# x, v, pos_emb and the result in the order of the kernel's loads and stores

## The chip, the core and the metric

One NeuronCore of a Trainium2 chip runs the whole program. Its engines are TensorE (PE; PEld is its weight load), VectorE (DVE), ScalarE (ACT), GpSimd (POOL) and SyncE (SP); in this kernel SP issues every DMA, one after the other. The metric is the time of one execution on the device, in microseconds. What the host does to the arrays before and after the execution is not in it.

## What is computed

A gated long convolution over the sequence (batch 4, sequence 12480, 128 channels) and then a token-wise network with a hard-swish between its two matrices:

```python
h_filt = (np.maximum(pos_emb @ w1, 0.0) @ w2) * window      # S x 128, window = exp(-0.01 pos)
u = x * v                                                   # B x S x 128
y = irfft(rfft(u, n=2*S) * rfft(h_filt, n=2*S))[:, :S]      # causal convolution over the sequence
a = (x * y).reshape(B * S, 128)
h = a @ w_in                                                # 128 -> 2048
out = (h * np.clip(h + 3.0, 0.0, 6.0) / 6.0) @ w_out        # 2048 -> 128
```

## The kernel before

The sequence is laid out as 196 rows of N1 = 64 positions (98 and 97 of them hold data, for the halves k = 0 and 1, called R[0] and R[1]); the Fourier transform over it is done by matmuls in stages. The program has three parts, one after the other.

**The filter (`Conv.filter`).** `pos_emb` is loaded with one of the 98 rows on each partition into the tile z (called `pt` there, the rows of k = 0 and k = 1 side by side). For 16 groups of NB = 4 positions `turned` transposes it on TensorE (L293, four transposes into one bank) and VectorE copies the bank out (L300), and `hidden` multiplies by w1 (L305) and applies ReLU on ScalarE (L306); a group is turned two groups ahead of its `hidden`. `spread` multiplies by w2 (L327) and by the window on VectorE (L335). Then come the first transform stage (L223, evicted at L235 and L233) and the second (L242), and the filter's spectra are stored to `hd` in memory (L351). All this is done for 64 of the 128 channels at a time. The tables `ftab`, `ctab`, `dtab` and the first pieces of x and v are loaded meanwhile.

**The convolution (`Conv.period`).** There are NG = 8 periods, each for 2 of the 4 sequences and G = 32 channels, and each has 25 chunks of up to four frequencies. A chunk runs `spectra` (L242, with a table piece `tab`), `swapped` (L474 and L475 on ScalarE, into the one bank of `sw`), `products` (L495 to L498 on VectorE with a filter piece `h`, then the sums L502 on GpSimd) and, two chunks later, `third_stage` (L517, copied out at L525). In between, periods 1 to 7 turn the period before back (`back`, L532, L136, L137; `fourth_stage`, L551, L557; `store`), and periods 0 to 6 run the first stage of the period after (`visit`, eight of them, L223 and L235).

For that first stage `gate_next` multiplies x by v on GpSimd (L426), and `load_next` loads the next x and v (L415). A load covers half the positions of one piece (98 rows of 32 positions by 32 channels), and each position's 32 channels are a run of 128 bytes in memory:

```python
part = slice(half * N1 // 2, (half + 1) * N1 // 2)
for t, src in ((xt, self.x), (vt, self.v)):
    for r0, r1 in ((0, 96), (96, R[k])):
        nc.sync.dma_start(t[r0:r1], self.rows(src, b, k, r0, r1)[:, part, d : d + G])
```

Each period makes eight such loads, four DMAs each. In the same queue of SP stand, for each chunk, two DMAs of `h` (L459, NH = 4 buffers) and one of `tab` (L446, NT = 7 buffers), each issued when a buffer comes free, and the stores of y (L567, L569). SP takes its rows strictly in the order of the program: a DMA that waits for its buffer, or for an earlier DMA on the same semaphore, holds all behind it.

**The network (`Moe`).** 98 tiles of 512 tokens; a tile's x and y are loaded (`load`), multiplied (`gate`), transposed by 32 x 32 blocks on VectorE (`turn`), put through both matrices by matmuls in three passes (`up`, L764 to L766; `down`, L799 to L803), transposed back (`finish`, L816) and stored. Its x load and its result store go through `copy`, by four DMAs of 32 partitions each (32 DMAs for a tile of leftover rows), in runs of 32 channels:

```python
for q in range(4):
    s = tile[32 * q : 32 * q + 32, cols].rearrange("r (n c) -> r n c", c=32)
```

## Time and profile before

| | |
|---|---|
| three runs | 3316.59, 3317.9 and 3318.12 us, median 3317.9 us |
| the profiled execution | 3315.44 us, of which 3313.7 us from the first to the last instruction |
| busy: PE, PEld | 3226.8 us (97%), 2764.7 us (83%) |
| busy: DVE, ACT, POOL | 2380.8 us (72%), 2400.2 us (72%), 2108.6 us (64%) |
| DMA packets | 972127, of which 841962 under 512 bytes; 296.41 MB |

The page is one execution. Its busy times are sums over three parts with different limits, so a part is read by itself: the filter stands in the first 171 us, the convolution up to about 1185 us, and the network after that. A matmul's end is modelled, so that a busy PE is not always one at its peak. The profiled execution is 2.5 us under the median of the runs.

### The profile page before, as it was taken

How to read it: one execution, taken by the hardware profiler on the slowest of the kernel's cores; microseconds unless marked ns; L12 is line 12 of the kernel's file. 1: busy time of each engine (PE TensorE's matmuls, PEld its weight loads, DVE VectorE, ACT ScalarE, POOL GpSimd, SP SyncE). 2: the span in 40 equal slices, each digit the busy share in tenths (PEclk: the TensorE clock that was granted, in tenths of full speed). 3: DMA queues.
4: the chain of work that ended last, by engine and by line, in shares of the span. 5: the costliest groups of instructions: out<-in, count | busy, mean ns of one | idle time of the engine just before them, and what ended most of it. 6: DMA issues, size and time to landing. Idle time of an engine off the chain costs nothing.

```text
span 3313.7 us, 54920 instructions
## 1 busy us (share of the span) xinstructions
PE 3226.8 (97%) x20346; PEld 2764.7 (83%) x20346; DVE 2380.8 (72%) x2837; ACT 2400.2 (72%) x3104; POOL 2108.6 (64%) x1243
## 2 busy tenths in 40 slices
PE   8988999999999999999999999999999999999999
PEld 7988888888888888888888888888888888888887
DVE  5545666666766667777777777777777777777776
ACT  2355666666667677778778787787878777777777
POOL 1166677676776546666666666666666666666666
PEclk9998999999999999999999999999999999999999
DMA  9789989989985522211211222112221112221121
GB/s 208 200 163 187 187 186 193 187 194 186 189 186 168 170 61 39 39 33 34 45 34 34 39 39 39 34 34 38 39 39 37 32 37 39 39 39 32 36 39 23
DMA packets 972127, 296.41 MB, mean 89 GB/s; under 512 B 841962, under 2 KB 938641, under 8 KB 970769
## 3 DMA queue, kind: packets, MB, share of 16 engines
q1 hardware_dynamic: 971860, 292.91, 42.1%
q8 instruction: 160, 2.62, 0.4%
q14 instruction: 107, 0.88, 0.1%
HBM read 224.49 MB, written 68.29 MB: 88 GB/s over the span
## 4 chain that ended last, share of the span: by engine, by line
PE 68%; POOL 0%; DVE 0%; issue 0%; ACT 0%
PE acc L803 11%; PE ph L764 11%; PE acc L800 11%; PE ph L765 11%; PE acc L799 11%; PE ph L766 11%; PE s L551 1%; PE ts L532 1%; PE s L517 1%; PE s L242 1%; PE s L532 0%; POOL pa L502 0%; DVE o L816 0%; ACT oT L806 0%; DVE wlo L137 0%
## 5 line engine op out<-in xcount | busy, mean ns | idle before, releaser
L788 POOL TENSOR_TENSOR glo<-g,ghi 128x1024 fp32r<-128x1024 f32 x588 | 1404.3, 2395 | 766.5 <-ACT ghi L786 766.3
L776 DVE SCALAR_TENSOR_TENSOR g<-r,ph 128x1024 f32<-128x1024 f32 (+1 forms) x784 | 949.5, 1211 | 411.1 <-ACT r L774 411.0
L774 ACT ACTIVATE r<-ph,three 128x1024 f32<-128x1024 f32 (+1 forms) x784 | 870.9, 1111 | 274.1 <-PE ph L766 274.0
L786 ACT CAST ghi<-g 128x1024 fp32r<-128x1024 f32 (+1 forms) x784 | 811.0, 1034 | 0.8 <-DVE g L776 0.7
L764 PE MATMUL ph<-xhi,win_hi 128*128 128x512 f32 (+1 forms) x1568 | 608.4, 388 | 0.0
L765 PE MATMUL ph<-xlo,win_hi 128*128 128x512 f32 (+1 forms) x1568 | 608.3, 388 | 0.0
L766 PE MATMUL ph<-xhi,win_lo 128*128 128x512 f32 (+1 forms) x1568 | 608.3, 388 | 0.0
L800 PE MATMUL acc<-ghi,wout_lo 128*128 128x512 f32 (+1 forms) x1568 | 608.0, 388 | 0.0
L799 PE MATMUL acc<-ghi,wout_hi 128*128 128x512 f32 (+1 forms) x1568 | 607.9, 388 | 0.0
L502 POOL TENSOR_TENSOR pa<-pa,pq 128x256 f32<-128x256 f32 (+1 forms) x400 | 312.5, 788 | 274.7 <-DVE pa L496 234.3
L803 PE MATMUL acc<-glo,wout_hi 128*128 128x512 f32 (+1 forms) x1568 | 481.2, 388 | 0.0
L764 PEld LDWEIGHTS ph<-xhi,win_hi 128*128 128x128 f32 x1568 | 294.3, 188 | 60.9 <-DVE g L776 0.2
L799 PEld LDWEIGHTS acc<-ghi,wout_hi 128*128 128x128 f32 x1568 | 294.4, 188 | 60.7
L765 PEld LDWEIGHTS ph<-xlo,win_hi 128*128 128x128 f32 x1568 | 294.5, 188 | 60.5
L766 PEld LDWEIGHTS ph<-xhi,win_lo 128*128 128x128 f32 x1568 | 294.4, 188 | 60.5
L800 PEld LDWEIGHTS acc<-ghi,wout_lo 128*128 128x128 f32 x1568 | 294.3, 188 | 60.4
L803 PEld LDWEIGHTS acc<-glo,wout_hi 128*128 128x128 f32 x1568 | 293.5, 188 | 60.9 <-POOL glo L788 0.7
L495 DVE TENSOR_TENSOR pq<-s,h 128x256 f32<-128x256 f32 (+1 forms) x200 | 84.2, 421 | 284.2 <-issue 106.3
L788 DVE TENSOR_TENSOR glo<-g,ghi 128x1024 fp32r<-128x1024 f32 x196 | 283.6, 1447 | 0.0
L223 PEld LDWEIGHTS ts<-ctab,u 98*64 98x64 f32 (+1 forms) x5120 | 229.4, 139 | 46.4 <-DVE wlo L137 24.9
L223 PE MATMUL ts<-ctab,u 98*64 98x99 f32 (+1 forms) x5120 | 246.8, 254 | 21.3 <-DVE wlo L137 20.8
L517 PE MATMUL s<-pa,tab 128*128 128x128 f32 x1694 | 240.9, 288 | 26.7 <-POOL pa L502 14.8
(72 smaller groups left out, 4060.0 us busy)
## 6 DMA issues: line engine op xcount, KB each, us to landing
tab<-in_g_tab SPq DMA_DIRECT2D x192, 256.0 KB
h<-hd SPq DMA_DIRECT2D x384, 128.0 KB
xt<-in_x SPq DMA_DIRECT2D x64, 384.0 KB
vt<-in_v SPq DMA_DIRECT2D x64, 384.0 KB
yd<-y SPq DMA_DIRECT2D x192, 128.0 KB
xt<-in_x SPq DMA_DIRECT2D x384, 64.0 KB
yt<-yd SPq DMA_DIRECT2D x96, 256.0 KB
out<-o SPq DMA_DIRECT2D x384, 64.0 KB
```

Source lines behind the costliest of these rows:

```text
L223: nc.tensor.matmul(tv[c * N1 : (c + 1) * N1, i, :K2], u[: R[k], 4 * j + i, :], self.ctab[: R[k], c * K2 : (c + 1) * K2], start=True, stop= ...
L502: nc.gpsimd.tensor_tensor(out=x, in0=x, in1=y, op=add)
L764: nc.tensor.matmul(ph[:, i, :ne], self.win_hi[:, sl], hi[:, :ne], start=True, stop=False)
L765: nc.tensor.matmul(ph[:, i, :ne], self.win_hi[:, sl], lo[:, :ne], start=False, stop=False)
L766: nc.tensor.matmul(ph[:, i, :ne], self.win_lo[:, sl], hi[:, :ne], start=False, stop=True)
L774: nc.scalar.activation(r[:, :, :ne], ph[:, :, :ne], AF.Relu, bias=self.three)
L776: nc.vector.scalar_tensor_tensor(out=g[:, :, :ne], in0=r[:, :, :ne], scalar=6.0, in1=ph[:, :, :ne], op0=ALU.min, op1=ALU.mult)
L786: nc.scalar.copy(ghi[:, :, :ne], g[:, :, :ne])
L788: e.tensor_tensor(out=glo[:, :, :ne], in0=g[:, :, :ne], in1=ghi[:, :, :ne].bitcast(F32), op=ALU.subtract)
L799: nc.tensor.matmul(a, self.wout_hi[:, f, :], ghi[:, i, :ne], start=(f == 0), stop=False)
L800: nc.tensor.matmul(a, self.wout_lo[:, f, :], ghi[:, i, :ne], start=False, stop=False)
L803: nc.tensor.matmul(a, self.wout_hi[:, f, :], glo[:, i, :ne], start=False, stop=(f == NFC - 1))
```

## The change

The host hands x, v and `pos_emb` over in the order in which the kernel's tiles hold them, x a second time (`xt`) in the order of the network's tiles, and takes the result in that order too.

- `by_groups`: x and v by period, piece and half, so that a half now is 16 channels with all 64 positions; a partition's share of a load is one run of 4096 bytes. The tile has the order of u, and both halves k have 98 rows (the rows beyond the sequence are zeros). The gate's output is no longer strided.
- `by_pairs`: `pos_emb` with 128 values (64 features of two positions) on the partitions. The transposes, their copies and the two memsets of the padding go; `hidden` reads the loaded tile. It is loaded in four pieces (4, 12, 16 and 32 positions), after w1 and ahead of `ident`.
- `by_tiles` and `from_tiles`: a tile's x load and its result store are one DMA of 128 partitions by 2048 bytes each. The y load is as before.

```diff
+def blocks(a):
+
+    b, s, d = a.shape
+    out = np.zeros((b, 2 * L, d), a.dtype)
+    out[:, :s] = a
+    return out.reshape(b, 2, R[0], N1, d)
+
+
+def by_groups(a):
+
+    a = blocks(a).reshape(B // GB, GB, 2, R[0], N1, D // G, 2, G // 2)
+    a = a.transpose(0, 5, 2, 1, 6, 3, 7, 4)
+    return np.ascontiguousarray(a).reshape(NG, 2 * GB, 2, R[0], G // 2, N1)
+
+
+def by_tiles(a):
+
+    a = blocks(a)
+    main = a[:, :, : 32 * NR].reshape(B, 2, NR, 32, N1 // 16, 16, 4, 32).transpose(0, 1, 2, 4, 6, 3, 5, 7)
+    main = main.reshape(-1, 128, 512)
+    rest = np.stack([a[i] for i in REST]).reshape(-1, 2, 32, 4, 32).transpose(3, 2, 0, 1, 4).reshape(128, -1)
+    pad = np.zeros((128, -rest.shape[1] % 512), a.dtype)
+    rest = np.concatenate([rest, pad], axis=1).reshape(128, -1, 512).transpose(1, 0, 2)
+    return np.ascontiguousarray(np.concatenate([main[:AT], rest, main[AT:]]))
+
+
+def from_tiles(t):
+
+    n = -(-len(REST) // 8)
+    main = np.concatenate([t[:AT], t[AT + n :]])
+    out = np.zeros((B, 2, R[0], N1, D), t.dtype)
+    out[:, :, : 32 * NR] = (
+        main.reshape(B, 2, NR, N1 // 16, 4, 32, 16, 32).transpose(0, 1, 2, 5, 3, 6, 4, 7).reshape(B, 2, 32 * NR, N1, D)
+    )
+    rest = t[AT : AT + n].transpose(1, 0, 2).reshape(4, 32, -1, 2, 32)[:, :, : len(REST)].transpose(2, 3, 1, 0, 4)
+    for i, a in zip(REST, rest.reshape(-1, N1, D)):
+        out[i] = a
+    return np.ascontiguousarray(out.reshape(B, 2 * L, D)[:, :S]).reshape(B * S, D)
+
+
+def by_pairs(a):
+
+    a = blocks(a[None])[0].reshape(2, R[0], N1 // 4, 2, 2, FO)
+    return np.ascontiguousarray(a.transpose(4, 5, 2, 0, 3, 1)).reshape(2 * FO, N1, R[0])
...
@@ -265,53 +307,25 @@
 
         flat = z.rearrange("p k c -> p (k c)")
 
-        pt = flat[: R[0], : 2 * N1 * FO].rearrange("p (k n i) -> p k n i", k=2, n=N1)
-        pos = [pos_emb[k * L : k * L + R[k] * N1, :].rearrange("(r n) i -> r n i", n=N1) for k in range(2)]
-
-        def load_pos(n0, n1):
-            for k in range(2):
-                nc.sync.dma_start(pt[:96, k, n0:n1, :], pos[k][:96, n0:n1, :])
-
-        nc.vector.memset(pt[96 : R[0], 1, :NB], 0.0)
-        nc.gpsimd.memset(pt[96 : R[0], 1, NB:], 0.0)
-        load_pos(0, NB)
-        nc.sync.dma_start(self.ident, ident_d)
-        for k in range(2):
-            nc.sync.dma_start(pt[96 : R[k], k], pos[k][96:])
+        pT = flat[:, : N1 * R[0]].rearrange("p (n r) -> p n r", r=R[0])
         for k in range(2):
             nc.sync.dma_start(w1bd[k * FO : (k + 1) * FO, k * FO : (k + 1) * FO], w1)
-        for n in ((NB, 8), (8, 16), (16, 32), (32, N1)):
-            load_pos(*n)
+        for n0, n1 in ((0, NB), (NB, 16), (16, 32), (32, N1)):
+            nc.sync.dma_start(pT[:, n0:n1, :], pos_emb[:, n0:n1, :])
+        nc.sync.dma_start(self.ident, ident_d)
         for k in range(2):
             nc.sync.dma_start(w2bd[k * FO : (k + 1) * FO, k, :], w2)
         nc.sync.dma_start(win, win_d)
         nc.sync.dma_start(self.ctab, self.c_tab)
 
-        def turned(n):
-            tp = self.bank("ptT")
-            for i in range(NB):
-                nc.tensor.transpose(
-                    tp[:, i * R[0] : (i + 1) * R[0]],
-                    pt[:, i // 2, n + i % 2 * 2 : n + i % 2 * 2 + 2, :].rearrange("p n i -> p (n i)"),
-                    self.ident[: R[0], : R[0]],
-                )
-            i = 2 * N1 * FO + n // NB % 4 * NB * R[0]
-            pT = flat[:, i : i + NB * R[0]]
-            nc.vector.tensor_copy(pT, tp[:, : NB * R[0]])
-            return pT
-
-        def hidden(n, pT):
+        def hidden(n):
             h1 = self.bank("h1")
-            nc.tensor.matmul(h1[:, : NB * R[0]], w1bd, pT, start=True, stop=True)
+            src = pT[:, n : n + NB, :].rearrange("p n r -> p (n r)")
+            nc.tensor.matmul(h1[:, : NB * R[0]], w1bd, src, start=True, stop=True)
             nc.scalar.activation(ht[:, n : n + NB, :].rearrange("p n r -> p (n r)"), h1[:, : NB * R[0]], AF.Relu)
 
-        pend = []
         for n in range(0, N1, NB):
-            pend.append((n, turned(n)))
-            if len(pend) > 2:
-                hidden(*pend.pop(0))
-        while pend:
-            hidden(*pend.pop(0))
+            hidden(n)
 
         for q in range(3):
             nc.sync.dma_start(ftab[:, 33 * q : 33 * q + 33, :], f_tab[:, 33 * q : 33 * q + 33, :])
...
@@ -407,25 +421,21 @@
             return
         g, i = divmod(self.n_loaded, 4 * GB)
         piece, half = divmod(i, 2)
-        k, b, d = self.place(g, piece)
-        xt, vt = ((xv or self.xv).tile([R[0], N1 // 2, G], F32, tag=f"{c}t", name=f"{c}t") for c in "xv")
-        part = slice(half * N1 // 2, (half + 1) * N1 // 2)
+        xt, vt = ((xv or self.xv).tile([R[0], G // 2, N1], F32, tag=f"{c}t", name=f"{c}t") for c in "xv")
         for t, src in ((xt, self.x), (vt, self.v)):
-            for r0, r1 in ((0, 96), (96, R[k])):
-                nc.sync.dma_start(t[r0:r1], self.rows(src, b, k, r0, r1)[:, part, d : d + G])
-        self.loaded.append((k, part, xt, vt, xv is None))
+            for r0, r1 in ((0, 96), (96, R[0])):
+                nc.sync.dma_start(t[r0:r1], src[g, piece, half, r0:r1])
+        self.loaded.append((half, xt, vt, xv is None))
         self.n_loaded += 1
 
     def gate_next(self):
 
         if self.loaded:
-            k, part, xt, vt, again = self.loaded.pop(0)
-            if part.start == 0:
+            half, xt, vt, again = self.loaded.pop(0)
+            if half == 0:
                 self.gated.append(self.up.tile([R[0], G, N1], F32, tag="u", name="u"))
-            u = self.gated[-1]
-            self.nc.gpsimd.tensor_tensor(
-                out=u[: R[k], :, part].rearrange("p g n -> p n g"), in0=xt[: R[k]], in1=vt[: R[k]], op=ALU.mult
-            )
+            u = self.gated[-1][:, half * G // 2 : (half + 1) * G // 2, :]
+            self.nc.gpsimd.tensor_tensor(out=u, in0=xt, in1=vt, op=ALU.mult)
             if again:
                 self.load_next()
 
...
-        self.tiles[16:16] = [REST[i : i + NB // 2] for i in range(0, len(REST), NB // 2)]
+        self.tiles[AT:AT] = [REST[i : i + NB // 2] for i in range(0, len(REST), NB // 2)]
         self.loaded, self.gated, self.ready, self.done = {}, {}, {}, None
 
...
     def columns(self, t):
         return 64 * len(self.tiles[t]) if self.is_rest(t) else 32 * self.NB
 
-    def places(self, arr, t):
-
-        NB, i = self.NB, self.tiles[t]
-        if self.is_rest(t):
-            for s, (b, k, r) in enumerate(i):
-                a = arr[b, k * L + r * N1 : k * L + (r + 1) * N1, :]
-                yield slice(64 * s, 64 * s + 64), a.rearrange("(h r) (q c) -> q r h c", r=32, c=32)
-        else:
-            b, k, q, n = i
-            a = arr[b, k * L + 32 * q * N1 : k * L + 32 * (q + 1) * N1, :]
-            yield slice(0, 32 * NB), a.rearrange("(r n) (q c) -> q r n c", n=N1, c=32)[:, :, n : n + NB, :]
-
-    def copy(self, tile, arr, t):
-
-        for cols, a in self.places(arr, t):
-            for q in range(4):
-                s = tile[32 * q : 32 * q + 32, cols].rearrange("r (n c) -> r n c", c=32)
-                if arr is self.x:
-                    self.nc.sync.dma_start(s, a[q])
-                else:
-                    self.nc.sync.dma_start(a[q], s)
-
     def is_rest(self, t):
...
@@ -709,7 +696,7 @@
         nc = self.nc
         xt = self.io.tile([128, 512], F32, tag="x", name="xt", bufs=3)
         y = self.io.tile([128, 512], F32, tag="y", name="yt", bufs=3)
-        self.copy(xt, self.x, t)
+        nc.sync.dma_start(xt, self.x[t])
         if self.is_rest(t):
             i = self.tiles[t]
             s = REST.index(i[0])
@@ -814,7 +801,7 @@
         ne = self.columns(t)
         o = self.io.tile([128, 512], F32, tag="o", name="o")
         nc.vector.transpose(out=o[:, :ne], in_=oT[:, :ne])
-        self.copy(o, self.out, t)
+        nc.sync.dma_start(self.out[t, :, :ne], o[:, :ne])
 
     def run(self):
         enter, tc = self.ctx.enter_context, self.tc
...
-_INS = ["x", "v", "pos_emb", "w1", "w2", "moe_w_in", "moe_w_out"]
-
-
 def kernel(**inputs):
     import concourse.bacc as bacc
     from concourse.bass_utils import run_bass_kernel_spmd
 
     nc = bacc.Bacc("TRN2", target_bir_lowering=False, num_devices=1)
     arrays, args = {}, []
-    given = {n: np.ascontiguousarray(inputs[n]) for n in _INS} | constants()
+    x = np.asarray(inputs["x"])
+    given = {
+        "x": by_groups(x),
+        "v": by_groups(np.asarray(inputs["v"])),
+        "xt": by_tiles(x),
+        "pos_emb": by_pairs(np.asarray(inputs["pos_emb"])),
+    }
+    given |= {n: np.ascontiguousarray(inputs[n]) for n in ("w1", "w2", "moe_w_in", "moe_w_out")} | constants()
     for name, a in given.items():
         if a.dtype == np.float64:
             a = a.view(np.uint64)
         arrays[f"in_{name}"] = a
         args.append(nc.dram_tensor(f"in_{name}", a.shape, mybir.dt.from_np(a.dtype), kind="ExternalInput").ap())
-    args.append(nc.dram_tensor("out", (B * S, D), F32, kind="ExternalOutput").ap())
+    args.append(nc.dram_tensor("out", given["xt"].shape, F32, kind="ExternalOutput").ap())
```

On SP the start of the program stands as follows before; z_79 is the tile that takes `pos_emb`, z_80 the table `ftab`.

```order
L273 DMA z_79<-in_pos_emb 96x256 x2
L278 DMA ident<-in_ident 128x128
L280 DMA z_79<-in_pos_emb 2x4096
L280 DMA z_79<-in_pos_emb 1x4096
L282 DMA w1bd<-in_w 64x64 x2
L273 DMA z_79<-in_pos_emb 96x256 x2
L273 DMA z_79<-in_pos_emb 96x512 x2
L273 DMA z_79<-in_pos_emb 96x1024 x2
L273 DMA z_79<-in_pos_emb 96x2048 x2
L286 DMA w2bd<-in_w 64x128 x2
```

And now, at the same place:

```order
L312 DMA w1bd<-in_w 64x64 x2
L314 DMA z_79<-in_pos_emb 128x392
L314 DMA z_79<-in_pos_emb 128x1176
L314 DMA z_79<-in_pos_emb 128x1568
L314 DMA z_79<-in_pos_emb 128x3136
L315 DMA ident<-in_ident 128x128
L317 DMA w2bd<-in_w 64x128 x2
```

Twelve DMAs of `pos_emb` have become four, and w1 has moved from behind the first of them to the front. On PE the same stretch is, before, a row of transposes between the products with w1:

```order
L293 MATMUL ptT<-ident,z_79 128x98 x12
L305 MATMUL h_149<-z_79,w1bd 128x392
L293 MATMUL ptT<-ident,z_79 128x98 x4
L305 MATMUL h_158<-z_79,w1bd 128x392
L293 MATMUL ptT<-ident,z_79 128x98 x4
```

and now those products alone:

```order
L324 MATMUL h_121<-z_79,w1bd 128x392
L324 MATMUL h_124<-z_79,w1bd 128x392
L324 MATMUL h_127<-z_79,w1bd 128x392
L324 MATMUL h_130<-z_79,w1bd 128x392
L324 MATMUL h_133<-z_79,w1bd 128x392
```

What has gone are 64 transposes of 98 columns; the 16 products are the same. In period 0 (its last chunks, with the piece of 3 frequencies) SP's queue reads, before:

```order
L415 DMA xt<-in_x 96x32x32
L415 DMA xt<-in_x 2x32x32
L415 DMA vt<-in_v 96x32x32
L415 DMA vt<-in_v 2x32x32
L459 DMA h<-hd_57 64x2x256 x2
L446 DMA tab<-in_g_tab 128x512
L459 DMA h<-hd_57 64x2x256 x2
L446 DMA tab<-in_g_tab 128x512
```

and now:

```order
L427 DMA xt<-in_x 96x1024
L427 DMA xt<-in_x 2x1024
L427 DMA vt<-in_v 96x1024
L427 DMA vt<-in_v 2x1024
L469 DMA h<-hd_57 64x2x256 x2
L456 DMA tab<-in_g_tab 128x512
L469 DMA h<-hd_57 64x2x256 x2
L456 DMA tab<-in_g_tab 128x512
```

No row has moved; the x and v rows have the same bytes in runs of 1024 values in place of 32 runs of 32.

## Rows read from the trace of the kernel before

**Rows 1.** Windows of periods 0, 4 and 7 and of the network.

```profile
165.00:295.00 130.00, 109.61 (x1222) 104.01 (x1218) 60.20 (x123) 65.82 (x124) 85.01 (x84) 0.92 0.92 173
...
677.00:805.00 128.00, 119.26 (x1134) 107.07 (x1133) 87.92 (x167) 85.05 (x159) 91.84 (x85) 0.97 0.92 191
...
1052.00:1131.00 79.00, 78.42 (x535) 71.97 (x534) 58.78 (x114) 59.80 (x107) 57.02 (x64) 1.00 0.55 161
1300.00:3200.00 1900.00, 1900.00 (x8428) 1575.09 (x8427) 1476.26 (x1231) 1510.39 (x1581) 1254.77 (x528) 1.00 0.20 37
```

The columns are: stretch, length, busy time and instructions of PE, PEld, DVE, ACT and POOL, the granted clock, the DMA share, GB/s.

**Rows 2.** Timeline of the first 45 us: start, duration, engine, line, count, idle before.

```profile
5.02 0.56 PE L293 MATMUL ptT<-ident,z 98*128 98x98 f32 x2 [5.02 <-DMA z<-in_pos_emb]
...
13.16 1.56 PE L305 MATMUL h<-z,w1bd 128*128 128x392 f32 x2
...
28.18 2.17 PE L305 MATMUL h<-z,w1bd 128*128 128x392 f32 x6
...
30.18 14.14 PE L327 MATMUL h<-w2bd,ht 128*98 128x128 f32 x128
```

**Rows 3.** Windows of the start, columns as in Rows 1.

```profile
10.00:15.00 5.00, 4.82 (x15) 3.05 (x16) 1.13 (x2) 0.73 (x2) 0.00 (x0) 1.00 0.99 258
...
25.00:30.00 5.00, 5.00 (x28) 3.32 (x26) 2.27 (x4) 2.73 (x6) 0.00 (x0) 1.00 1.01 429
```

**Rows 4.** SP's timeline in period 0.

```profile
199.08 3.10 SPq L415 DMA_DIRECT2D xt<-in_x  x2
202.23 2.70 SPq L415 DMA_DIRECT2D vt<-in_v  x2
...
206.42 0.54 SPq L446 DMA_DIRECT2D tab<-in_g_tab  x1
```

**Rows 5.** PE's timeline, three second-stage groups at the starts of periods 1 and 6.

```profile
272.00 1.06 PE L242 MATMUL s<-z,tab 128*128 128x128 f32 x8
...
276.83 2.05 PE L242 MATMUL s<-z,tab 128*128 128x128 f32 x8 [2.77 <-DMA tab<-in_g_tab]
...
929.60 2.04 PE L242 MATMUL s<-z,tab 128*128 128x128 f32 x8 [2.23 <-DMA tab<-in_g_tab]
```

**Rows 6.** ACT's timeline, `swapped` of single chunks (one L474 each).

```profile
172.41 0.56 ACT L474 COPY sw<-s 64x512 f32<-64x512 f32 x1 [2.08 <-PE s L242]
...
212.44 0.56 ACT L474 COPY sw<-s 64x512 f32<-64x512 f32 x1 [1.59 <-DVE pa L498]
217.34 0.56 ACT L474 COPY sw<-s 64x512 f32<-64x512 f32 x1
220.60 0.56 ACT L474 COPY sw<-s 64x512 f32<-64x512 f32 x1 [1.59 <-DVE pa L498]
...
273.43 0.56 ACT L474 COPY sw<-s 64x512 f32<-64x512 f32 x1 [0.64 <-DVE pa L498]
...
301.97 0.56 ACT L474 COPY sw<-s 64x512 f32<-64x512 f32 x1
...
793.34 0.56 ACT L474 COPY sw<-s 64x512 f32<-64x512 f32 x1 [1.24 <-DVE pa L498]
...
816.62 0.56 ACT L474 COPY sw<-s 64x512 f32<-64x512 f32 x1
...
920.81 0.56 ACT L474 COPY sw<-s 64x512 f32<-64x512 f32 x1 [1.24 <-DVE pa L498]
...
944.16 0.56 ACT L474 COPY sw<-s 64x512 f32<-64x512 f32 x1
```

**Rows 7.** Waits from 165 to 295 us: total, times, longest.

```profile
PE s L242 <- DMA tab<-in_g_tab: 13.2, 8, 3.1
```

**Rows 8.** Timeline of the end: the last instruction of an engine.

```profile
3308.46 0.71 DVE L816 STREAM_TRANSPOSE o<-oT 128x512 f32<-128x512 f32 x1 [3.93 <-ACT oT L806]
```

**Rows 9.** Instructions of the result's store (L703) from 3200 us: ns min/median/max.

```profile
L703 SPq DMA_DIRECT2D out<-o x24: 316/488/1452, 3214.9 to 3310.6; - x24
```

**Rows 10.** The gate's group of instructions: count, busy us, mean ns, idle before.

```profile
L426 POOL TENSOR_TENSOR u<-xt,vt 98x1024 f32<-98x1024 f32 (+1 forms) x64 | 154.0, 2407 | 142.1 <-PE ts L223 90.1 <-DMA vt<-in_v 50.5 <-POOL u L426 1.5
```

More of the change, by code (lines that the diff above doesn't have):

```diff
@@ L45 @@
 REST = [(b, k, r) for b in range(B) for k in range(2) for r in range(32 * NR, R[k])]
+AT = 16
 ON_DVE = (2, 6)
@@ L91, in constants, with hyena_moe @@
     return {k: np.ascontiguousarray(a, dtype=np.float32) for k, a in out.items()}
+def blocks(a):
[29 more added lines that the diff above has]
+    return np.ascontiguousarray(a.transpose(4, 5, 2, 0, 3, 1)).reshape(2 * FO, N1, R[0])
 @with_exitstack
-def hyena_moe(ctx, tc, x, v, pos_emb, w1, w2, w_in, w_out, c_tab, d_tab, f_tab, g_tab, win_d, ident_d, out):
+def hyena_moe(ctx, tc, x, v, xt, pos_emb, w1, w2, w_in, w_out, c_tab, d_tab, f_tab, g_tab, win_d, ident_d, out):
     nc = tc.nc
@@ L109, in hyena_moe @@
     ident = const.tile([P, P], F32, name="ident")
-    def rows(t, b, k, r0, r1):
-        a = t[b, k * L + r0 * N1 : k * L + r1 * N1, :]
-        return a.rearrange("(r n) d -> r n d", n=N1)
     left, right = ExitStack(), ExitStack()
     with tc.manual_schedule():
-        conv = Conv(tc, nc, left, right, x, v, c_tab, d_tab, g_tab, ident, hd, yd, ye, rows, weights)
+        conv = Conv(tc, nc, left, right, x, v, c_tab, d_tab, g_tab, ident, hd, yd, ye, weights)
         conv.filter(pos_emb, w1, w2, f_tab, win_d, ident_d)
@@ L123, in hyena_moe @@
         left.close()
-        moe = Moe(ctx, tc, nc, x, wd, yd, ye, out)
+        moe = Moe(ctx, tc, nc, xt, wd, yd, ye, out)
         conv.last_turn(moe)
@@ L192, with __init__ @@
 class Conv:
-    def __init__(self, tc, nc, left, right, x, v, c_tab, d_tab, g_tab, ident, hd, yd, ye, rows, weights):
+    def __init__(self, tc, nc, left, right, x, v, c_tab, d_tab, g_tab, ident, hd, yd, ye, weights):
         self.tc, self.nc, self.left, self.right = tc, nc, left, right
-        self.x, self.v, self.g_tab, self.ident, self.hd, self.yd, self.rows = x, v, g_tab, ident, hd, yd, rows
+        self.x, self.v, self.g_tab, self.ident, self.hd, self.yd = x, v, g_tab, ident, hd, yd
         self.c_tab, self.d_tab, self.weights, self.ye = c_tab, d_tab, weights, ye
@@ L657, in __init__ @@
         self.ctx, self.tc, self.nc = ctx, tc, nc
-        self.x, self.yd, self.ye = x, yd, ye
-        self.out = out.rearrange("(b s) d -> b s d", b=B)
+        self.x, self.yd, self.ye, self.out = x, yd, ye, out
         P = 128
@@ L865 @@
     r = run_bass_kernel_spmd(nc, [arrays], core_ids=[0])
-    return r.results[0]["out"]
+    return from_tiles(r.results[0]["out"])
```

## Prediction

> **What bounds the kernel now.** I read the windows by stage first, since the program's parts have different limits. In the network TensorE is busy for 1900.00 of 1900 us with 8428 matmuls at a granted clock of 1.00, while the DMA engines are at 0.20 [rows 1]: 225 ns per matmul, and nothing that a load or a store does there can be worth anything until the last tile. In period 0 of the convolution it is the other way round: the DMA share is 0.92, TensorE has 109.61 of 130 us, and its granted clock is 0.92 on average, so that some of that busy time runs at the lower of its two levels (1.2 in place of 2.4 GHz). In period 7, which loads no x and v, the DMA share is 0.55 and the clock 1.00 [rows 1].
>
> Next I read the start in order of time. TensorE begins at 5.02 us, as soon as the first `pos_emb` lands, and alternates transposes and products with w1 until `spread` begins at 30.18 us [rows 2]. From there to the first chunk's copy at 172.41 [rows 6] I found no wait of TensorE's that is worth a term, so a `spread` that begins earlier moves all of this stretch.
>
> Then SP's timeline in period 0, because a late table is TensorE's largest wait there (13.2 us in eight waits, [rows 7]). One load of x and v keeps SP for 3.10 + 2.70 us, and a `tab` DMA for 0.54 us [rows 4]; its rows stand back to back (199.08 + 3.10 is 202.18, the next begins at 202.23), which says that tables come late because SP comes to them late. Last, ScalarE's `swapped`: with one bank for `sw`, a chunk can't copy before the one ahead of it has been through VectorE. Undisturbed that makes 3.26 us for a chunk and 4.90 us for one with a visit (217.34 to 220.60, 212.44 to 217.34, [rows 6]). This ring, not TensorE, is what a chunk of period 0 is measured against.
>
> **The change, part by part.**
>
> *The start.* 64 transposes go from TensorE, and 16 copies from VectorE. What is left is 16 products, 2.17 us for three (x6 in the row; 28.18 to `spread` at 30.18 is 2.00), so 0.65 to 0.67 us each, and twice that at the clock's lower level: one took 1.56 us at 13.16 [rows 2]. The stretch is then bound by data. `pos_emb` is 98 x 128 x 64 x 4 bytes = 3.21 MB. Before, 10 to 15 us ran at 258 GB/s and the long runs of `ftab` at 429 GB/s [rows 3]; the new pieces have runs of 1.6 to 12.5 KB, which lie between, so the bytes take 7.5 to 12.4 us. With the first piece at about 5.5 us (w1's two DMAs are now ahead of it) the last 1.6 MB lands between 12 and 17.5 us. At the slow rate eight groups follow it: 17.5 + 8 x 0.66 = 22.8 us, a gain of 7.4. At the fast rate TensorE is the bound: some eight groups at the lower level (5.5 to 16 us; before, the level rose between 13.16 and 28.18) and eight at the upper one, 21.3 us, a gain of 9; with an earlier rise 19, a gain of 11. I take **8.5 us**, and 4 to 11 as bounds (the 4 is the second rival). `ident`, w2, `win` and `ctab` now stand behind `pos_emb`, are small, and are needed at `spread` at the earliest; `ftab` is needed behind `spread`'s 14.14 us and the first stage that follows it, and is 6.3 MB, 15 us at 429 GB/s. Hidden, all of them.
>
> *The loads of x and v in period 0.* A load's four DMAs fall to at most 4 x 0.54 = 2.2 us of SP's time (the `tab` row has more rows per DMA than they), from 5.8: eight per period free 29 us of SP. The bytes stay, in runs of 4096 in place of 128 bytes. What this gives back is read from the ring, not from TensorE's waits. From the first chunk's copy at 172.41 to the first of period 1 at 273.43 are 25 steps in 101.0 us [rows 6]. Clean they are 16 x 3.26 + 8 with a visit at 4.9 + 2.5 (the chunk of three frequencies, three quarters of a step) = 93.9 us: **7.1 us** lost. The next five steps, where TensorE waits for tables at 276.83 for 2.77 us and then needs 2.05 us for eight matmuls that took 1.06 before the wait [rows 5], reach from 273.43 to 301.97, 28.5 us; the same five in period 5 take 23.3 us (793.34 to 816.62, [rows 6]): **5.3 us** lost. Together 12.4; bounds 2 (tables stay late) and 15.
>
> *The same loads in periods 1 to 6.* Here too a table comes late at a period's start, 2.23 us at 929.60 [rows 5]. But that period's first five steps take 920.81 to 944.16 = 23.35 us, against 23.28 us where nearly nothing was waited for [rows 6]. The wait lies beside the ring and beside work that TensorE has to do anyway. I take **0**, and 5 us (two such waits in the six periods) as its upper bound; below nothing I see no price but the clock's (fourth rival).
>
> *The gate on GpSimd.* Its output is now contiguous. It takes 2407 ns [rows 10], and no row shows it without the stride. It lies beside the ring, so **0** whichever way it goes.
>
> *The network.* x loads and result stores are hidden under a TensorE that never waits. Only the end counts: the last transpose ends at 3309.17 us [rows 8], the span at 3313.7, so 4.5 us for four DMAs issued at 488 ns each [rows 9] and their landing. One issue in place of four saves three issues, 1.46 us, if the bytes keep up. I take **1.3 us**, bounds 0 and 2.
>
> *Sum.* 8.5 + 12.4 + 0 + 0 + 1.3 = 22.2 us. The profiled execution took 3315.4 us (3313.7 and 1.7 around them), which gives 3293.2; the median of the runs is 2.5 us above the profiled one, so I forecast **3295 us**, with 3286 to 3303 as this case's own range.
>
> **The rivals.**
>
> *Tables stay late.* SP's queue keeps its order, and a load of x and v still waits for the gate to free its buffer, and for earlier DMAs on its semaphore. If that and not the issue time holds the tables, period 0 gives 2 us: 3305. Against it: in period 7, with the tables and filters alone, TensorE has 78.42 of 79 us [rows 1], so none is waited for, and SP's rows in period 0 stand back to back.
>
> *A cold start.* Before, the transposes kept TensorE at work while `pos_emb` came in: 4.82 of 5 us between 10 and 15 us [rows 3]. After, it works only as pieces land, and the lower level may last through all 16 groups: 16 x 1.31 = 21 us from 5.5, `spread` at 26.5, a gain of 3.7 in place of 8.5, which makes 3300. The Trainium skill, "TensorE: Matmul & The Clock Gate", Part 1, has this as its rule: the slow clock is the default and sustained work releases it, so work taken off an early TensorE delays the release. The trace shows the rise but not what becomes of it without the transposes.
>
> *The late tables of periods 1 to 6 count after all.* Then another 5 us, and with a clock that falls less often 5 more: 3285 to 3290. For it: the matmuls behind the long wait ran at the lower level there too, 2.04 us for eight [rows 5]. Against: the five steps around it took as long as elsewhere.
>
> *The clock falls more often.* TensorE's short gaps at the periods' starts, waits for ScalarE, VectorE and GpSimd that the change doesn't touch, bring the lower level in some places and not in others. Period 4 runs at a mean of 0.97, which is 3.8 us of full-speed time lost in 128; period 0 at 0.92 [rows 1]. If the work slides so that periods 1 to 6 fall to 0.94 as well, 0.03 x 128 x 6 = 23 us and the gain is gone; at 0.92 the kernel takes 3295 + 38 = 3333. It decides at 0.94. Nothing that I see favours more gaps over fewer.
>
> *No gain.* The start's gain is lost at a wait that I don't see (the filter's stores and reloads before period 0), and tables stay late: 3315.
>
> **How the numbers follow.** Forecast 0.58 (3295), late tables 0.10 (3305), cold start 0.12 (3300), more from the later periods 0.13 (3287), clock 0.03 (3318 to 3333), no gain 0.04 (3315). The range 3282 to 3307 leaves out the last two and the tails of the others, under 2 in 10. A run can't tell less than 0.2% (6.6 us) from no change: faster means under 3311.3. Faster is the first four cases, 0.93 less a little for their tails, 0.92; the same 0.06; slower 0.02.
>
> **What would show it.** `spread` beginning at 20 to 23 us in place of 30.18 (at 26 or more, the cold start). The copies of the first chunk of period 0 and of period 1 some 94 us apart in place of 101.0, the next five in 23 to 24 us, no wait for `tab` over 0.5 us in period 0, its clock near 1, and a DMA share of some 0.65. The distance between the first chunks of periods 5 and 6 unchanged at about 127.5 us (793.34 to 920.81, [rows 6]). The network's 1900 us window unchanged. The end from the last transpose to the end of the span 3 us. The forecast is wrong if SP's rows for x and v stay at several microseconds each, or if the ring's step is not what limits period 0 once tables are there.

## The result and the profile after

The changed kernel took 3281.15 us (median of four runs, 3278.28 to 3288.01) beside 3317.24 us (four runs, 3310.94 to 3318.12) of the kernel before: a ratio of 0.9898, 95% interval 0.9879 to 0.9918. It is faster, as forecast, but by 36 us where 22 were forecast; the time lies 0.85 us below the low end of the range. The profiled execution took 3281.17 us, its span 3279.4 where before it was 3313.7.

The page after: the span, busy times, granted clock and DMA share in 40 slices, packets, and the queue of SP's DMAs.

```profile
span 3279.4 us, 53881 instructions
...
PE 3203.3 (98%) x20282; PEld 2743.5 (84%) x20282; DVE 2368.2 (72%) x2820; ACT 2398.6 (73%) x3104; POOL 2105.2 (64%) x1242
...
PEclk9999999999999999999999999999999999999999
DMA  6687667766665511111111110111011111111010
...
DMA packets 198899, 296.72 MB, mean 90 GB/s; under 512 B 31559, under 2 KB 128110, under 8 KB 197614
...
q1 hardware_dynamic: 198638, 293.27, 30.0%
```

The megabytes are those of before (296.41), in a fifth of the packets (972127 before). The next rows are windows of the kernel after, columns as in [rows 1]: two of the start, then the counterparts of those of periods 0, 4 and 7 and of the network.

```profile
5.00:10.00 5.00, 4.66 (x7) 2.21 (x8) 0.00 (x0) 1.04 (x3) 0.00 (x0) 1.00 1.01 395
10.00:15.00 5.00, 4.58 (x13) 2.25 (x13) 0.00 (x0) 2.94 (x6) 0.00 (x0) 1.00 1.04 390
155.00:285.00 130.00, 115.94 (x1352) 109.47 (x1349) 68.73 (x141) 76.59 (x144) 94.86 (x93) 0.99 0.79 198
667.00:795.00 128.00, 119.10 (x1146) 107.22 (x1145) 89.67 (x169) 85.95 (x162) 93.48 (x85) 0.99 0.68 193
1020.00:1099.00 79.00, 78.42 (x535) 71.94 (x534) 59.22 (x115) 59.49 (x108) 57.16 (x63) 1.00 0.55 160
1300.00:3200.00 1900.00, 1900.00 (x8429) 1575.06 (x8427) 1475.11 (x1229) 1509.56 (x1580) 1255.62 (x527) 1.00 0.11 37
```

In the 130 us around period 0 TensorE now has 1352 matmul records in place of 1222 [rows 1], at a clock of 0.99 in place of 0.92. Period 7 and the network are as before. In the two rows of the start the clock column can't be read: it says 1.00, while one and the same product takes 1.31 us early in this stretch and 0.66 later. The level at the start is therefore read from durations. SP's timeline in period 0, which answers to [rows 4]:

```profile
209.91 0.67 SPq L427 DMA_DIRECT2D xt<-in_x  x2
210.63 0.75 SPq L427 DMA_DIRECT2D vt<-in_v  x2
211.48 1.24 SPq L469 DMA_DIRECT2D h<-hd  x2
212.81 0.54 SPq L456 DMA_DIRECT2D tab<-in_g_tab  x1
```

A load of x and v takes 1.4 us of SP in place of 5.8, and TensorE has no wait for `tab` at all in this stretch, where [rows 7] had 13.2 us. SP's DMA rows from the first chunk's copy of period 0 to that of period 1 add up to 88.7 of 101.0 us before and to 55.4 of 92.0 after (summed over its timeline). So SP now waits where it hardly did: these are its longest waits in total from 160 to 300 us, before, then after.

```profile
SPq L459 <- DVE pa L498: 3.2, 3, 2.3
```

```profile
SPq L469 <- DVE pa L508: 28.0, 16, 10.4
```

The start, and ScalarE's `swapped` of the first chunk of period 0, of period 1, and of the fifth step behind it (L484 after is L474 in [rows 6]); the last row is the end, as [rows 8]:

```profile
4.95 1.64 PE L324 MATMUL h<-z,w1bd 128*128 128x392 f32 x2 [4.95 <-DMA z<-in_pos_emb]
6.93 6.87 PE L324 MATMUL h<-z,w1bd 128*128 128x392 f32 x14 [0.34 <-DMA z<-in_pos_emb]
...
14.22 5.50 PE L324 MATMUL h<-z,w1bd 128*128 128x392 f32 x16 [0.42 <-DMA z<-in_pos_emb]
...
19.56 0.71 PE L341 MATMUL h<-w2bd,ht 128*98 128x128 f32 x5
...
161.79 0.56 ACT L484 COPY sw<-s 64x512 f32<-64x512 f32 x1 [2.08 <-PE s L284]
...
253.75 0.56 ACT L484 COPY sw<-s 64x512 f32<-64x512 f32 x1 [0.64 <-DVE pa L508]
...
277.19 0.56 ACT L484 COPY sw<-s 64x512 f32<-64x512 f32 x1
...
3275.76 0.71 DVE L803 STREAM_TRANSPOSE o<-oT 128x512 f32<-128x512 f32 x1 [3.93 <-ACT oT L793]
```

`spread` begins at 19.56 us in place of 30.18, and the first chunk moves by the same 10.62 us (172.41 to 161.79). From there the distances of ScalarE's copies (of each period's first chunk, and of the last chunk of period 7) divide the 34.3 us between the two spans, without a remainder. A step is the distance from one chunk's copy to the next:

```
stretch                  before    after    gained
start to first chunk     172.41   161.79     10.62
period 0                 101.02    91.96      9.06
period 1                 134.41   128.30      6.11   (its first five steps 28.54, 23.44: 5.10)
periods 2 to 5           512.97   506.05      6.92
periods 6 and 7          211.12   211.43     -0.31
network and the end     2181.77  2179.86      1.91   (the end 4.5, 2.9: 1.6)
```

### The profile page after: what moved, and what is told of

The parts are those of the page before. It is cut to its first block, busy times and chain, and to the rows that moved or that the text cites. A ratio compares the mean times of both kernels' runs of the same rounds, so it can differ in the third digit from the quotient of the medians.

```text
span 3279.4 us, 53881 instructions
## 1 busy us (share of the span) xinstructions
PE 3203.3 (98%) x20282; PEld 2743.5 (84%) x20282; DVE 2368.2 (72%) x2820; ACT 2398.6 (73%) x3104; POOL 2105.2 (64%) x1242
## 4 chain that ended last, share of the span: by engine, by line
PE 69%; POOL 0%; DVE 0%; issue 0%; ACT 0%
PE acc L790 11%; PE ph L751 11%; PE ph L753 11%; PE ph L752 11%; PE acc L786 11%; PE acc L787 11%; PE s L561 1%; PE ts L542 1%; PE s L527 1%; PE s L284 1%; PE s L542 0%; POOL pa L512 0%; DVE o L803 0%; ACT oT L793 0%; DVE wlo L179 0%
## 5 line engine op out<-in xcount | busy, mean ns | idle before, releaser
L527 PEld LDWEIGHTS s<-pa,tab 128*128 128x128 f32 x1694 | 213.9, 196 | 63.6 <-POOL pa L512 43.8
```

Source lines behind the costliest of these rows:

```text
L527: nc.tensor.matmul(t[:, i * 128 : (i + 1) * 128], tab[:, i, :], a[:, i].rearrange("p s g -> p (s g)"), start=(n == 0), stop=(n == len(term ...
```

## The experiments

Twelve runs, of eleven kernels and of the changed one a second time, each timed beside the kernel before on the same chip. Its medians there were 3322.68 us beside the three with one part and the one with work ahead of w1, 3316.82 beside the 12-row pieces, the full copies, GpSimd's queue and the first dummies in the periods, and 3322.76 beside the second profile, half the copies and the last two with dummies; ratios are to these.

**One part at a time.** Three kernels take one part of the diff each into the kernel before.

> The kernel before with pos_emb alone laid out by the host (no transposes, no copies of them); x, v and the result as before. Pass-through theory: spread begins at 19.6 us in place of 30.18, the first chunk's copy of period 0 moves by the same 10.6 us to 161.8, everything behind keeps its length (period 0 101.0 us, the five steps behind it 28.5, the end 4.5), and the time falls by 10.6 us to about 3306.5. Rival, lost at a later wait: the first chunk stays near 172 and the time at 3317. On periods 2 to 5, which together took 513.0 us before and 506.1 after: if the loads of x and v give that gain, they stay at 512 to 514 here; if it is only where the program's phase puts the low clock stretches, they may come out anywhere from 505 to 522.

It took 3309.72 us, 0.9960 (0.9946 to 0.9974). `spread` begins at 20.22 us, the first chunk's copy comes at 162.47, so 9.9 us earlier; period 0 keeps 102.61 us, and 6.4 us of waits for `tab` are still there. By the medians the time fell by 13.0 us, so the start's gain isn't lost on the way; between the two profiled executions the span fell by 6.2 us alone, since periods 2 to 5, whose loads are those of before, took 519.2 us here and 513.0 there.

> The kernel before with the conv stage's x and v alone laid out by the host (and so a gate without strides); pos_emb, the network's loads and the stores as before. Theory that these loads give all of the gain behind the start: spread still at 30.2 us, period 0 in 92 us in place of 101.0, the next five steps in 23.4 in place of 28.5, periods 2 to 5 together 506 us in place of 513.0, and a time of about 3317 - 9.1 - 6.1 - 7 = 3295. Rival, the gain of the later periods belongs to the phase that the earlier start gave: 513 us for periods 2 to 5 and a time of 3302. Rival, tables come late for another reason: waits for tab stay and period 0 is over 98 us.

It took 3294.85 us, 0.9919 (0.9905 to 0.9934), with no wait for `tab` in period 0. Period 0 is 91.90 us, the next five steps 22.04, periods 2 to 5 506.7. So with the start of before the loads of x and v bring all that the changed kernel gains in the periods; the earlier start isn't needed for it (that a start can undo part of it is seen in the run with work ahead of w1, below). By the medians they gain 27.8 us, between the two profiles 20.8: the profiled execution of the kernel before took 3315.44 us, 7 us under its median here. That the time fell on the 3295 expected is in part luck, since the kernel that it was counted from stood 5 us higher.

> The kernel before with the network's x and the result alone laid out as tiles; pos_emb and the conv stage's x and v as before. Theory that only the end counts: the stretch from the last transpose's end to the span's end falls from 4.5 to 2.9 us, the 1900 us of the network stay, and the time falls by 1.6 us to 3315.6, within what a run can tell from no change. Rival, the network's loads cost something in the convolution or the hand-over to the network: 3311 or below.

It took 3321.15 us, 0.9996 (0.9987 to 1.0006): no difference that can be told, as expected. In its trace the stretch behind the last transpose is 2.9 us (4.5 before). Its periods, whose code is that of before, took 518.2 us for 2 to 5 where the kernel before had 513.0 in its profile. Profiles with one and the same code there differ by up to 6 us.

**Why the tables came late: SP's time or the engines' load.** Four kernels part the two.

> The changed kernel with each load of x and v cut into pieces of 12 rows: 18 DMAs in place of 4, so the same bytes in the same runs of 4096 bytes, but some 18 x 0.28 = 5 us of SP's time for a load in place of 2 (before: 5.8). Theory that SP's issue time is what held the tables: the waits for tab come back, period 0 goes from 92 to 98 to 102 us, the five steps behind it from 23.4 to 26 or more, and the time rises by 8 to 15 us to 3289 to 3296. Rival, the load of the DMA engines (their share 0.92 before, 0.67 after) held them: the share stays at 0.67, period 0 stays at 92 us and the time at 3281.

```diff
-            for r0, r1 in ((0, 96), (96, R[0])):
+            for r0 in range(0, R[0], 12):
+                r1 = min(r0 + 12, R[0])
                 nc.sync.dma_start(t[r0:r1], src[g, piece, half, r0:r1])
```

It took 3367.88 us, 1.0164 (1.0148 to 1.0179), far more than I expected, because the later periods lost too (551.1 us for 2 to 5). SP's timeline, TensorE's waits from 160 to 300 us (total, times, longest), and the window of its period 0:

```profile
186.35 3.47 SPq L428 DMA_DIRECT2D xt<-in_x  x9
189.87 3.44 SPq L428 DMA_DIRECT2D vt<-in_v  x9
```

```profile
PE s L284 <- DMA tab<-in_g_tab: 20.2, 8, 6.6
```

```profile
168.75:278.52 109.77, 91.99 (x1002) 87.49 (x1001) 48.33 (x100) 55.94 (x106) 69.84 (x70) 0.91 0.54 161
```

A load is 6.9 us of SP, SP's rows fill 92.7 us of period 0, the tables are late by 20.2 us, and period 0 takes 109.8 us, with the DMA engines at a share of 0.54. In the changed kernel the share of period 0 was 0.82, so fuller engines are not what made these tables late.

> The changed kernel with a copy from DRAM to DRAM behind each load's DMAs of x and of v (0.8 MB each in 16 runs of 50 KB, so 1.6 MB and two short issues more for a load; what is copied is never read): it puts the DMA engines' share in periods 0 to 5 back to 0.9 or above with little of SP's time. Theory that SP's issue time held the tables: period 0 stays within 2 us of 92 and waits for tab stay short; 3281 to 3286. Rival, the engines' load held them: waits for tab and h come back, period 0 is 98 us or longer, 3292 or more.

```diff
                 nc.sync.dma_start(t[r0:r1], src[g, piece, half, r0:r1])
+            nc.sync.dma_start(
+                self.junk[0 if src is self.x else 1],
+                src[g, piece].rearrange("h r q n -> (h r q n)").rearrange("(p m) -> p m", p=16),
+            )
```

It took 3326.28 us, 1.0029 (1.0017 to 1.0041): the rival came, and by more than its 3292. The share in period 0 is 0.98, the waits for `tab` are 16.1 us, period 0 is 101.86 us. SP itself waits here for DMAs to land (8.5 and 6.6 us of waits for the two copies ahead of `h` loads, from 160 to 300 us), which it did not in the kernel before. So engines that are full hold the tables too; but a share of 0.98 is above that of before, and the next run halves the copies.

> As the run with copies from DRAM to DRAM, with half as much of it (0.4 MB behind x and 0.4 MB behind v): the engines' share in period 0 comes to about 0.9, where it was before the change (0.89), in place of 0.98. Theory that before the change SP's issue time and not the engines' load held the tables: waits for tab come to under 5 us and period 0 to 92 to 95 us. Rival, a share of 0.9 is enough to hold them: 13 us of waits for tab and period 0 at 99 us or more.

It took 3280.99 us, 0.9883 (0.9866 to 0.9899), as fast as the changed kernel. The windows of period 0, before the change, after it, and in this run, and this run's waits of TensorE for tables from 160 to 300 us:

```profile
172.41:273.43 101.02, 87.20 (x1002) 82.09 (x1001) 48.40 (x100) 55.70 (x105) 69.79 (x70) 0.97 0.89 171
161.79:253.75 91.96, 82.86 (x1002) 78.49 (x1001) 48.41 (x100) 55.53 (x106) 69.64 (x70) 1.00 0.82 203
161.01:253.11 92.10, 82.87 (x1002) 78.50 (x1001) 48.36 (x100) 55.47 (x105) 69.64 (x70) 1.00 0.94 267
```

```profile
PE s L286 <- DMA tab<-in_g_tab: 3.0, 2, 2.0
```

A share of 0.94, higher than the 0.89 of period 0 before, and still 92.1 us and two short waits; SP's rows fill 63.4 us of it. With the run of 12-row pieces this shows that period 0 was held by SP's issue time and not by the engines' load. One rival is left: these copies have long runs, and the many packets of 128 bytes that stood on the engines before are not in them. The next run keeps those packets.

> The kernel before with the DMAs of x and v issued from GpSimd's queue in place of SP's; layout, bytes and runs of 128 bytes as before. Theory that SP's issue time held the tables: SP is free of some 5.8 us eight times a period, period 0 falls from 101.0 toward 92 us if GpSimd's additions (the pa tiles) are not held up by the issues in their turn, and the time falls by some 10 to 15 us to 3303 to 3308. Rival, the load of the DMA engines held them: the share stays at 0.92, period 0 stays at 100 to 103 us. A third way: GpSimd, which adds the products of each chunk, is itself late by what the issues take (5 us or more for a load), and the kernel is slower than 3322.

It took 3420.61 us, 1.0317 (1.0299 to 1.0335): the third way. TensorE has no wait for `tab` left in period 0, with the runs of 128 bytes and a share of 0.85 still there, but a load takes 1.93 + 1.92 us of GpSimd, and the products that it adds come late. TensorE's longest waits from 211 to 331 us:

```profile
PE s L517 <- POOL pa L502: 23.2, 10, 5.9
```

Period 0 takes 119.2 us, and begins only at 211.29, 39 us later than before, since the filter's gates and loads share that queue too. That the tables are in time speaks against the rival of the packets, but doesn't exclude it, since a longer period also gives them more time.

The Trainium skill, "Perfetto Trace Analysis", DMA Optimizations, says that balancing DMAs over the engines that can issue them may help where generating descriptors is the bottleneck. The tables' waits agree with the diagnosis; the time does not agree with the remedy, since here the other queue belongs to an engine that TensorE waits for.

**What changes the later periods.** TensorE's timeline in period 3, where it waits for a `ts` bank that VectorE frees, before, then after:

```profile
614.88 2.91 PE L223 MATMUL ts<-ctab,u 97*64 97x99 f32 x32 [1.88 <-DVE wlo L137]
617.72 2.08 PE L517 MATMUL s<-pa,tab 128*128 128x128 f32 x8
```

```profile
589.19 1.59 PE L265 MATMUL ts<-ctab,u 97*64 97x99 f32 x32 [1.87 <-DVE wlo L179]
590.71 1.16 PE L527 MATMUL s<-pa,tab 128*128 128x128 f32 x8
```

The same wait, and behind it the lower of the clock's two levels before and the upper one after. These are steps 16 to 18 of the period, as windows before and after:

```profile
607.80:626.97 19.17, 16.77 (x138) 15.16 (x138) 12.14 (x22) 11.19 (x22) 12.77 (x12) 0.82 0.94 185
```

```profile
582.13:598.58 16.45, 14.06 (x138) 12.54 (x138) 12.04 (x22) 11.00 (x21) 12.34 (x11) 1.00 0.68 192
```

I took this for chance, and took a second profile of the same kernel.

> The changed kernel once more, as it is, for a second profile of it. Theory that the gain of periods 2 to 5 (506 us in place of 513) is where the clock's low stretches fall and differs between executions of one kernel: their sum comes out elsewhere between 505 and 516 us, with period 0 at 92.0 again. Rival, that gain belongs to the changed loads and is fixed: 506 us again, P3 to P5 126.2 us each.

It took 3279.42 us, 0.9877 (0.9862 to 0.9892), and the rival was right: periods 2 to 5 took 505.0 us, and 3 to 5 126.27, 126.27 and 126.25. Lengths of steps 16 to 18 in periods 1 to 5, worked out from ScalarE's copies:

```
kernel                          P1     P2     P3     P4     P5   P2 to P5 in all
before                       19.39  18.05  19.17  19.42  18.05    513.0
pos_emb alone                19.31  18.06  18.07  18.05  18.06    519.2
network alone                19.13  18.06  19.47  18.05  19.46    518.2
after                        19.16  18.04  16.45  16.43  16.43    506.1
after, second profile        18.04  16.44  16.45  16.45  16.43    505.0
x and v alone                19.36  18.04  16.46  16.44  16.45    506.7
after, half the copies       16.46  17.94  18.03  19.36  18.02    511.0
after, work ahead of w1      19.43  18.07  19.43  18.06  19.36    515.7
```

A length near 18 us or more marks the lower level behind this wait. With the old loads it stands in all fifteen periods shown. With the new loads alone it stands in one or two of five, but in four of five where half the copies ride along, and in all five in the last row, which is the next run.

> The changed kernel with 16 small matmuls on zeros (128x64, their result is never read) ahead of the first product with w1, and the last piece of pos_emb in two halves. Theory that the first groups' lower clock level (1.31 us a group up to 10.5 us, 0.66 behind it) is what bounds the start: the level rises before or within the first groups, spread begins at 16.5 to 17.5 us in place of 19.56, and the time falls by 2 to 3 us from 3281. Rival, the arrival of pos_emb bounds the start: TensorE waits for the pieces and spread stays at 19 to 19.6 us. Rival, the dummies are too short to bring the rise forward: groups at 1.31 us up to 10.5 us as before, 19.56.

```diff
+        warm = sp.tile([P, 64], F32, name="warm")
+        nc.gpsimd.memset(warm, 0.0)
+        wps = self.bank("warm")
+        for i in range(16):
+            nc.tensor.matmul(wps[:64, :64], warm, warm, start=True, stop=True)
         pT = flat[:, : N1 * R[0]].rearrange("p (n r) -> p n r", r=R[0])
...
-        for n0, n1 in ((0, NB), (NB, 16), (16, 32), (32, N1)):
+        for n0, n1 in ((0, NB), (NB, 16), (16, 32), (32, 48), (48, N1)):
```

It took 3281.20 us, 0.9875 (0.9861 to 0.9890): the changed kernel's time. At its start the theory holds: TensorE's timeline shows the dummies and ScalarE's the groups behind them, 0.66 us apart from the second one on where no piece is waited for (1.3 us in the changed kernel, up to 11.21).

```profile
0.94 3.68 PE L314 MATMUL warm<-warm 128*64 128x64 f32 x32 [0.94 <-POOL warm L311]
5.05 0.90 PE L329 MATMUL h<-z,w1bd 128*128 128x392 f32 x2 [0.43 <-DMA z<-in_pos_emb]
...
17.24 3.00 PE L346 MATMUL h<-w2bd,ht 128*98 128x128 f32 x26
```

```profile
7.84 0.50 ACT L330 ACTIVATE ht<-h 128x392 f32<-128x392 f32 x1 [1.36 <-PE h L329]
8.50 0.50 ACT L330 ACTIVATE ht<-h 128x392 f32<-128x392 f32 x1 [0.16 <-PE h L329]
9.16 0.50 ACT L330 ACTIVATE ht<-h 128x392 f32<-128x392 f32 x1 [0.16 <-PE h L329]
```

`spread` begins at 17.24 us, and the first chunk's copy comes at 159.47, 2.32 us earlier; what the dummies and the halved piece each give of this was not run apart. But periods 2 to 5 of this execution lose 9.6 us to the lower level, at steps 16 to 18 and behind them, with loads that are the changed kernel's. It is the slowest of this kernel's four, which took 3276.85 to 3285.04 us.

**Holding the clock.** Two kernels and a combination fill TensorE's waits with dummy matmuls.

> The changed kernel with dummy matmuls (ident by ident, 128x128) in the waits at the start of periods 1 to 7: 8 ahead of the third stage of chunk 0 and 14 ahead of that of chunk 2, some 0.12 us each, written to the s3 bank that the real matmuls then overwrite; no DMA is touched. Theory that the clock's low stretches are what varies in the later periods: the low stretch some 13 us into each of periods 1 to 6 goes (the fifth step falls from about 10.5 to 9 us or less), the periods 2 to 5 fall from 506 to 498 to 502 us, and the time falls by 6 to 10 us to 3271 to 3275. Rival, the lower level costs nothing there because the ring sets the pace: no change, 3281. Rival, the dummies lie on the path: 22 x 0.12 = 2.6 us for each of seven periods, 3295 or more.

```diff
         t = self.bank("s3")
+        if g and c in (0, 2):
+            for i in range(8 if c == 0 else 14):
+                nc.tensor.matmul(t[:, :128], self.ident, self.ident, start=True, stop=True)
```

It took 3287.33 us, 0.9916 (0.9900 to 0.9933), some 6 us or more above the changed kernel's medians, though the intervals of the two ratios overlap. I had mis-sized the dummies: a matmul leaves two records in the trace, so that one costs some 0.25 us (28 records took 3.39 us), not 0.12. The level held where they stand (granted clock 1.00 from 521.9 to 528.2 us, against 0.76 from 521 to 528 in the changed kernel). But the first eight steps of period 3 took 37.59 us in place of 38.07, so the lower level there had cost only half a microsecond: the ring sets the pace. Period 7, which has no such wait, lost 2.95 us to the dummies, and steps 16 to 18 of period 3 came to 17.88 us in place of 16.45, at a clock of 0.91 from 582.8 to 601: a low stretch stands now where it costs more, as it does in four of the periods 1 to 5.

> The changed kernel with 28 dummy matmuls (ident by 29 columns of ident) behind the second tile of the fifth visit of each period, into columns of that tile's bank that nothing reads: they lie in the 1.87 us in which TensorE waits for a ts bank. No DMA is touched. Theory that the lower level behind this wait is what makes steps 16 to 18 of a period take 18.0 to 19.4 us in place of 16.45: all of periods 1 to 5 take 16.4 to 16.6 us there, and the time falls by some 4 us where the undisturbed kernel loses least (19.16 and 18.04 in periods 1 and 2 of the profiled execution) and by 10 where it loses most, to 3271 to 3277. Rival, the dummies hold up the copies of that tile and the ring behind them: 16.45 becomes 17.5 or more, 3284 or above. Rival, they are too few to hold the level: 18.0 to 19.4 stay, 3281.

```diff
+        if self.ps is not None and (piece, j) == (2, 1):
+            for i in range(28):
+                nc.tensor.matmul(tv[:, i % 4, K2:], self.ident, self.ident[:, K2:], start=True, stop=True)
         col = piece * G + 4 * j
```

It took 3350.18 us, 1.0088 (1.0073 to 1.0103): the first rival, and by so much that nothing is learned of the theory. The dummies were far too long: TensorE's timeline of period 3 has 10.77 us for them, in a wait of 1.87.

```profile
614.89 10.77 PE L274 MATMUL ts<-ident 128*128 128x29 f32 x56
625.59 2.91 PE L265 MATMUL ts<-ctab,u 97*64 97x99 f32 x32
```

> The dummies ahead of the first product with w1 and the halved last piece of pos_emb of the earlier run, and those behind the second tile of the fifth visit, in one kernel. Theory: the start's 2.3 us (first chunk at 159.5 in place of 161.8) and steps 16 to 18 at 16.45 us in every period, 3270 to 3276. Rival: what the start gains is lost where the clock falls next (steps 21 to 23, 38.4 to 40.1 us in place of 37.1 for the last seven steps), 3279 to 3284.

It took 3348.47 us, 1.0082 (1.0067 to 1.0097), with the same 10 us in every period; its first chunk comes at 159.88 us, so the start's gain is there a second time. No kernel that I ran beats the changed one by more than a run can tell.

## Why the prediction fell short

- **What bounds.** Right. The network's window did not move, period 0 was measured by the ring, and the gain came from the start, the tables and the end.
- **The start, 8.5 us.** The mechanism was right, the size was low: 10.62. Data at the slow rate did not bound it: the windows from 5 to 15 us show 395 and 390 GB/s where I had bounded by 258 [rows 3], and TensorE waited for pieces only 0.34 and 0.42 us. The level rose near 11 us, earlier than the 16 that I took, so that four groups ran low (ScalarE's first four copies lie 1.3 us or more apart, up to 11.21 us, the next ones 0.66) and not eight.
- **Period 0, 7.1 us, and the five steps behind it, 5.3.** The cause was right, and the runs with 12-row pieces and with half the copies show it. The two terms gave 9.06 and 5.10. The first was mis-sized by the clean period: I priced all eight visits at 4.90 us, and three of them came at 4.27 or 4.28 and one at 4.12, so that a clean period is 91.96 us and not 93.9.
- **The loads in periods 1 to 6, 0 us.** This is the term that failed. Periods 2 to 5 gave 6.92 us, and the rest of period 1 behind its first five steps 1.01. The step that went wrong is "the wait lies beside the ring": I looked at one wait at a period's start, which indeed gives nothing (the first eight steps of periods 2 to 6 took 187.6 us before and 190.0 after), and not at what the clock does in steps 16 to 18, where the gain lies (74.7 us before and 67.4 after, in periods 2 to 5). Its size is not sharp: against the 518 and 519 us of the two other profiles with the old loads it would be 12 to 13 us. I had it as a rival, "count after all", with 0.13.
- **The gate, 0 us.** Right: 2390 ns in place of 2407 [rows 10], unseen in the time.
- **The end, 1.3 us.** It gave 1.6.
- **The rivals.** Late tables fell (no wait for them). The cold start fell: the sixteen groups did not stay at the lower level, and the rule that I cited for it does not give 3300 here. The Trainium skill, "TensorE: Matmul & The Clock Gate", Part 1, says that activity releases the slow clock; the run with work ahead of w1, where the level was up from the second group on, agrees with that; in the changed kernel the level rose near 11 us, behind the products alone. The clock's rival did not come: the changed kernel's clock falls less often (a mean granted clock of 0.991 to 0.996 in its eight runs, of 0.986 to 0.991 in the 33 of the kernel before beside the experiments). That it exists, at under half of the 23 us that I priced, is seen in the 9.6 us that one execution lost with the same loads.

**What stays open.** The runs show that the changed loads and the upper level in steps 16 to 18 go together in the three profiles with no work added (from period 3 on, in one from period 2), that no profile with the old loads has it there, and that a start 2.3 us earlier, or half the copies, undid most of it. What decides behind which of two like waits the level falls was not isolated. A rival that no run tested is that the place of the wait in time decides, and the loads only through the lengths of the periods: in the changed kernel's first profile the low stretches of periods 3 to 6 begin at 523.0, 649.3, 775.6 and 901.9 us, 126.3 apart, and the periods are 126.2 long, so that each repeats the one before. There periods 2 to 6 have a low stretch at their fifth step (granted clock 0.79 from 393 to 401 us, 0.83 from 898 to 908), where it costs nearly nothing, and I can't say from these runs why the sixteenth step is then spared in most of them.

## What to carry to other kernels

Ask of a late transfer whether its queue was free to issue it, before asking whether the engines were free to move it: rows that stand back to back on the issuing queue are the mark (88.7 of 101.0 us here), and a share of the DMA engines of 0.94 was no bottleneck by itself. Price a recovered stall by what the stage's own step gives back, from steps of each kind counted one by one, and look at the clock of the whole stage as well as at the wait that you remove. A few microseconds gained ahead of a stage with a varying clock can't be told by a time alone; the distances between the same instructions in two traces show them.

## What the runs showed of the hardware

- The same 1.87 us wait was followed by the lower clock level (32 records in 2.91 us) or by the upper one (1.59), in the same place of the same program.
- In the run with dummies behind the second tile the clock fell while TensorE's records stand without a gap: its busy time from 620 to 625.6 us, in the midst of the 29-column dummies, is 5.60 of 5.60 us, the granted clock 0.50, and the 32 records behind them took 2.91 us.
- The issue time follows the number of DMAs and of runs in them, not of bytes: the same 0.8 MB cost SP 1.4 us in 4 DMAs, 6.9 in 18 DMAs of the same runs of 4096 bytes, and 5.8 in 4 DMAs of runs of 128 bytes. GpSimd's queue took 3.85 us for the last.
